# Row maxima beside the mlp in pairs of key blocks, and attention turns of six score tiles

## The chip, the cores and the metric

The kernel runs on one core of one Trainium2 chip. A core has five engines with a queue each: PE (TensorE, matrix products; its weight loads are shown apart as PEld), DVE (VectorE), ACT (ScalarE), POOL (GpSimd) and SP (SyncE, which here only starts transfers). Each queue runs in order, and they wait for one another through semaphores. PE writes to PSUM, 128 partitions by 8 banks of 512 f32 numbers. The metric is the device time of one execution in microseconds (us); lower is better. The inputs are f32. Most products are done in fp32r with each operand split into a high part (h) and a remainder (l), as three products hh + hl + lh.

## The reference

```python
x = A_x                                              # 1 x 2048 x 448
g = sigmoid((x * gate_w).sum(-1, keepdims=True))
# a: attention of 16 heads of 28
qkv = (x @ wqkv) split into q, k, v by heads
a = softmax(q @ k.T * 28 ** -0.5) @ v  (all heads side by side)  @ wo
# b: an mlp per token, 448 -> 1792 -> 448
y = layernorm(x)
b = gelu_tanh(y @ w1 + b1) @ w2 + b2
out = g * a + (1 - g) * b                            # 1 x 2048 x 448
```

Both halves read the same x; B_x is not used.

## The kernel before

Sizes: S = 2048 tokens in NC = 4 chunks of CH = 512 (TPC = 4 tiles of 128 each); 16 heads in NG = 4 sets of four; NF = 14 blocks of 128 hidden units. A "group" n = 0..15 is a set of heads and a chunk of queries, (g, c) = divmod(n, 4). The four heads j of a set lie on partitions 32j to 32j + 27, so that matmuls of four heads use four separate row groups of PE and can run side by side.

Stages, in PE's order, which is written out by hand for the whole kernel:
- q, k, v (L168, L184) to DRAM as high part and remainder; LayerNorm's statistics, turned to rows by two transposes (`ln_turn`, L212 to L214), each copied by DVE before it is stored.
- the mlp: for each chunk c, `mlp1(f)` for 14 blocks (11 products of 512 columns each, L451; then the gelu on ACT twice, L454 and L455, for the rounded and the full value, and the remainder `hl` on POOL, L456), then `mlp2(c, i)` for four token tiles (14 x 3 products of 448 columns, L463 to L466, a copy on ACT and a store). Its sums lie in banks 0 and 1. Weights are fetched, copied on ACT and subtracted during chunk 0 (`load_w1`, `load_w2`); the next chunk's normalised x is made by `ln_apply` on POOL and ACT. The order on ACT, DVE, POOL and SP is the scheduler's in this stage.
- the attention, in which all four other engines keep the order of the text: 256 steps (16 groups by 16 key tiles of 128) of four score tiles (four heads, each 128 keys by 512 queries), 1024 units u in turns of U = 5. `scores` (L620) issues three products for each of the first three units (banks 0 to 2, L629), an exp over the three banks (L634, ACT), then the same for the other two (banks 3 and 4). Behind them stand the p·v products (L658, f32, bank 7) of the steps whose four exps were in earlier turns: one step, or two in every fourth turn. After a group's last step `finish` divides by the softmax's sum; from the last set of heads on, `project` (L525 to L527) and `gated` follow in bank 6.

The exp needs the maximum of each row of scores beforehand; it is subtracted as a 29th row of the score products. The class `RowMax` computes it: per group 64 matmuls of 28 rows (128 queries by 512 keys, high parts only, L321) into a bank, and `reduce_max` on DVE, one or two banks at a time (L301, L303). A `close` turns a group's result (16 columns) and stores it to `ms`; `load_qm(n)` brings it into the 29th row and first issues whatever is missing. The 1040 units (16 x 65) are spread over PE's order by `Filler`: 476 of them beside the mlp, six at a time in banks 2 to 7 ("a visit"), counted out in slots of one product; the rest in the attention, up to three a turn in banks 5 and 6. In the mlp the keys lie in `khr`, loaded block by block with four transfers (`load_khr`, L381).

Of the kernel before, what the change touches and what calls it, by code (L numbers as in the profile page):

```python
# [30 lines left out]
MLP_MAX = 476  # L31
MLP_G = MLP_MAX // 260
MG = 6
FS = 4
LQ = 12
STEPS = (2, 5, 7, 8, 9, 10)
# [3 lines left out]
def kernel(ctx: ExitStack, tc: tile.TileContext, xt, wqk, wv, wo, xk, w1, b1, w2, b2,  # L40
# [7 lines left out]
    sel = const.tile([P, P], F32, name="sel")  # L48
# [16 lines left out]
    one_t = const.tile([S // P, P], F32, name="one_t")  # L65
    nc.vector.memset(one_t, 1.0)
    nc.sync.dma_start(ones, one_t)

# [15 lines left out]
    def staged(width):  # L84
        return my.tile([P, CH], F32, name="r", bufs=3)[:, :width]

    def load_w1(f):
        r = staged(CH)
        nc.sync.dma_start(r, w1[f].rearrange("p t x -> p (t x)"))
# [20 lines left out]
    def ln_fetch(c, t):  # L110
        lnx[c, t] = staged(CH)
        nc.sync.dma_start(lnx[c, t], xt[t, :, c * CH:(c + 1) * CH])
# [12 lines left out]
    with tc.tile_pool(name="qx", bufs=2) as qx, tc.tile_pool(name="qo", bufs=3) as qo, \  # L125
# [67 lines left out]

        def ln_stats(i):
            x = qx.tile([P, 2, D], F32, name="bxr")
            nc.sync.dma_start(x, xk[2 * i:2 * i + 2].rearrange("t p d -> p t d"))
# [22 lines left out]
        for c in range(NC):  # L219
            for m in range(NM):  # L220
                if c == 0:
                    if m + 1 < NM:
                        load_wqk(m + 1)
                    if m == 1:
                        for t, s in ((ident, ident_d), (sel, sel_d), (b1s, b1)):
# [11 lines left out]
                if c == 0 and m in (3, 5):  # L237
                    ln_stats(m // 4)
                if c == 1 and m == 1:
                    ln_rows(0, TPC)  # L240
                if c == 1 and m == 5:
                    ln_turn(0, TPC)
                if c == 1 and m == 6:
                    ln_load(0)
                if c == 1 and m >= 4 or c == 2 and m < 3:
                    ln_stats(m - 2 if c == 1 else m + 5)
                if c == 2 and m in (0, 1, 2, 4):
                    ln_fetch(0, (0, 1, 2, 2, 3)[m])
                if c == 2 and 3 <= m < 6 or c == 3 and m == 0:
                    ln_apply(0, m - 3 if c == 2 else 3)  # L250
# [4 lines left out]
                if c == 3 and m < 3:  # L255
# [513 lines left out]
```

## Time and profile before

| | |
|---|---|
| median of 3 runs | 1148.91 us (1144.49 to 1150.78) |
| the profiled execution | 1146.98 us |
| its span (first to last instruction) | 1145.2 us |
| granted TensorE clock, mean | 0.991 |
| PE busy | 1116.6 us, 98%, 8136 matmuls |
| DVE, ACT, POOL busy | 731.6, 635.9, 331.0 us |
| first and last L451 | 126.5 and 444.0 us |
| first L629, last L658 | 486.5 and 1130.1 us |

Durations below are of that one execution. A row of the groups reads: line, engine, operation, output<-input by the program's names with shapes and count; then busy us in all and mean ns of one; then the engine's idle us just before it and what ended them. A row of the timeline: start, duration, engine, line, operation, names, shapes, number merged into the row, and in brackets the idle time before. Matmul ends are modelled, and a matmul of f32 operands (L658) leaves two records, so that a step of four heads shows eight. What the engines are worth in a stage is read from stretches of that stage.

### The profile page before, as it was taken

The page shows a single profiled execution, that of the slowest core. Times are in us where ns is not written, and L with a number is a line of the kernel's source. Part 1 is how long each engine was busy: PE and PEld are TensorE (multiplying, and loading weights), DVE is VectorE, ACT ScalarE, POOL GpSimd, SP SyncE. Part 2 cuts the span into 40 slices and gives each one's busy share as a digit, 9 for nine tenths or more (in the row PEclk, how much of TensorE's full clock was granted, in tenths as well). Part 3 has the DMA queues.
Part 4 walks back from the last instruction along what each step waited for, and adds up shares of the span by engine and source line. Part 5 has one row for each costly group of instructions (what it writes and reads, how often), then busy time and mean ns, then how long its engine had stood idle before and what let it go on. Part 6 is the DMA issues. An engine that isn't in the chain of part 4 may idle for free.

```text
span 1145.2 us, 19823 instructions
## 1 busy us (share of the span) xinstructions
PE 1116.6 (98%) x8136; PEld 678.4 (59%) x8136; DVE 731.6 (64%) x1033; ACT 635.9 (56%) x668; POOL 331.0 (29%) x355
## 2 busy tenths in 40 slices
PE   6999989999999999989999999999999999999998
PEld 4778867777767777744444444444444444454556
DVE  3433287888878888666676766676676667646103
ACT  5324551132033032067887878878787887848463
POOL 4043367146044032011123012311222123444250
PEclk9999999999999999989999999999999999999999
DMA  8878643002100014062101211111121003002201
GB/s 269 277 217 303 208 141 88 25 9 68 47 23 18 25 30 114 25 168 72 30 12 36 52 40 40 36 27 39 31 64 36 18 19 91 12 25 68 66 26 49
DMA packets 53519, 84.35 MB, mean 74 GB/s; under 512 B 8676, under 2 KB 28660, under 8 KB 52628
## 3 DMA queue, kind: packets, MB, share of 16 engines
q1 hardware_dynamic: 49236, 76.96, 22.5%
q0 software_dynamic: 4192, 6.12, 2.1%
q8 instruction: 64, 1.05, 0.4%
q14 instruction: 27, 0.22, 0.1%
HBM read 56.40 MB, written 26.49 MB: 72 GB/s over the span
## 4 chain that ended last, share of the span: by engine, by line
PE 89%; DMA 4%; POOL 3%; DVE 2%; issue 1%; ACT 1%; SPq 0%; POOLq 0%; ACTq 0%; DVEq 0%
PE bank L658 22%; PE bank L629 20%; PE bank L321 15%; PE bank L451 10%; PE bank L168 4%; PE bank L466 4%; PE bank L463 4%; PE bank L464 4%; PE bank L184 2%; PE bank L525 1%; DMA bxr<-in_xk 1%; PE bank L526 1%; PE bank L527 1%; DMA xraw<-in_xt 1%; POOL hl L456 1%
## 5 line engine op out<-in xcount | busy, mean ns | idle before, releaser
L634 ACT ACTIVATE pt<-bank 128x1536 f32<-128x1536 f32 (+1 forms) x410 | 484.6, 1234 | 155.9 <-PE bank L629 155.9
L301 DVE TENSOR_REDUCE mx<-bank 128x1 f32<-128x512 f32 x624 | 413.4, 687 | 174.9 <-PE bank L321 161.0
L658 PE MATMUL bank<-pt,vg 128*32 128x512 f32 x2048 | 263.7, 606 | 0.0
L303 DVE TENSOR_REDUCE mx<-bank 128x2 f32<-128x1024 f32 x200 | 235.4, 1219 | 41.1 <-PE bank L321 41.0
L321 PE MATMUL bank<-khi,qd 28*128 28x512 f32 x512 | 241.6, 479 | 0.3 <-DVE mx L301 0.2
L321 PEld LDWEIGHTS bank<-khi,qd 28*128 28x128 f32 x512 | 92.3, 181 | 148.3 <-DVE mx L301 107.0
L629 PE MATMUL bank<-qh,klo 28*128 28x512 f32 x1024 | 179.0, 395 | 0.0
L629 PE MATMUL bank<-qh,khi 29*128 29x512 f32 x768 | 161.8, 484 | 0.3 <-ACT h L469 0.3
L451 PE MATMUL bank<-y,w1f 128*128 128x512 f32 x616 | 153.2, 400 | 0.6 <-ACT h L455 0.6
L451 PEld LDWEIGHTS bank<-y,w1f 128*128 128x128 f32 x616 | 113.8, 190 | 36.1 <-issue 12.5
L629 PE MATMUL bank<-ql,khi 28*128 28x512 f32 x768 | 133.6, 393 | 0.0
L456 POOL TENSOR_TENSOR hl<-h,hh 128x512 fp32r<-128x512 f32 x56 | 72.5, 1295 | 172.0 <-ACT h L455 160.8
L658 PEld LDWEIGHTS bank<-pt,vg 128*32 128x32 f32 x2048 | 45.7, 108 | 84.6 <-issue 83.1
L629 PEld LDWEIGHTS bank<-qh,klo 28*128 28x128 f32 x1024 | 90.2, 186 | 4.2
L321 PE MATMUL bank<-khr,qd 28*128 28x512 f32 x512 | 80.7, 467 | 7.3 <-DVE mx L303 4.2
L541 POOL DMA_DIRECT2D lt<-ob x15 | 10.8, 723 | 265.7 <-DVE ob L540 265.7
L466 PE MATMUL bank<-w2h,hl 128*128 128x448 f32 x224 | 85.1, 380 | 1.9 <-POOL hl L456 1.9
L469 ACT ACTIVATE h<-bank 128x448 f32<-128x448 f32 x16 | 8.7, 543 | 140.4 <-PE bank L466 140.4
L629 PEld LDWEIGHTS bank<-qh,khi 29*128 29x128 f32 x768 | 63.3, 183 | 36.8 <-ACT pt L634 32.1
L463 PE MATMUL bank<-w2h,hh 128*128 128x448 f32 x224 | 84.7, 378 | 0.3 <-ACT hh L454 0.3
L454 ACT ACTIVATE hh<-bank,b1s 128x512 fp32r<-128x512 f32 x56 | 38.4, 685 | 81.9 <-PE bank L451 81.8
L464 PE MATMUL bank<-w2l,hh 128*128 128x448 f32 x224 | 82.3, 368 | 0.0
(100 smaller groups left out, 1237.0 us busy)
## 6 DMA issues: line engine op xcount, KB each, us to landing
qk<-hl SPq DMA_DIRECT2D x28, 512.0 KB
xraw<-in_xt SPq DMA_DIRECT2D x16, 256.0 KB
vs<-vt SPq DMA_DIRECT2D x16, 256.0 KB
r<-in_xt SPq DMA_DIRECT2D x16, 256.0 KB
rc<-rls POOLq DMA_DIRECT2D x60, 64.0 KB, 2.2
bxr<-in_xk SPq DMA_DIRECT2D x8, 448.0 KB
r<-in_w SPq DMA_DIRECT2D x14, 256.0 KB
gbs<-h SPq DMA_DIRECT2D x16, 224.0 KB
```

What stands on the lines that cost most here:

```text
L168: nc.tensor.matmul(ps, a, b, start=(i == 0), stop=(i == len(ops) - 1))
L301: nc.vector.reduce_max(self.mx[:, c0:c0 + 1], bank[:, b0], axis=AX)
L303: nc.vector.reduce_max(self.mx[:, c0:c1 + 1:c1 - c0], bank[:, b0:b1 + 1], axis=AX)
L321: nc.tensor.matmul(bank[:, b], self.qds[self.n][r, i * P:(i + 1) * P], khi[self.n // NC][r, k * 512:(k + 1) * 512], start=True, stop=True)
L451: nc.tensor.matmul(ps, a, b, start=(i == 0), stop=(i == len(ops) - 1))
L456: nc.gpsimd.tensor_sub(hl[f], h, hh[f].bitcast(F32))
L463: nc.tensor.matmul(a, hh[f][:, sl], w2h[f], start=(f == 0), stop=False)
L464: nc.tensor.matmul(a, hh[f][:, sl], w2l[f], start=False, stop=False)
L466: nc.tensor.matmul(a, hl[f][:, sl], w2h[f], start=False, stop=(f == NF - 1))
L629: nc.tensor.matmul(bank[:, u % U], a[r, k * P:(k + 1) * P], b[r], start=(i == 0), stop=(i == 2))
L634: nc.scalar.activation(t, bank[:, b:b + len(units)], AF.Exp, scale=SCALE)
L658: nc.tensor.matmul(pv[32 * j:32 * j + 32, :], vg[n // NC][:, k, 32 * j:32 * j + 32], probs.pop(4 * step + j), start=(k == 0), stop=(k == N ...
```

## The change

- `RowMax.visit` replaces the visits in the mlp. The keys are taken two blocks of 512 at a time, a and b: `load_khr` now puts K_a - K_b in the place of block a (two transfers per head into a staging buffer of the pool `rl` and into `khr`, and a subtraction on POOL) and K_b in the place of b. For three units at a time, three matmuls give a - b in banks 2 to 4 and three give b in banks 5 to 7. ACT computes relu(a - b) into a buffer of `rl` (three buffers), and one DVE instruction forms b + relu(a - b), which is max(a, b), and its maximum along the row. A group is 32 such pairs and a close.
- NX = 11 of the 16 groups (704 of 1024 maxima) are done so, in visits of three units (MG) from block FS = 6 of the first chunk on. The other five stay in the attention as before, one bank (6) at a time.
- The attention's turns have six units, two triples, in banks 0 to 5, with at most two row maxima each: one ahead of the first triple and one behind the second's products; one only in the turn after a projection (`projected`). STEPS, which counts turns after a group's end, is adapted, and six buffers hold the exps.
- In `mlp1` the gelu runs once, and DVE copies it to `hh`.
- In the mlp ACT, DVE, POOL and SP now keep the order of the text. Weights and x have fetches apart from their splits, in two staging buffers (four until chunk 0 is over).
- `ln_turn` makes both transposes before one copy; statistics are fetched earlier; loads of `sel`, `ones` and of the keys of sets 1 to 3 (`load_khi`) move.

The core of the diff:

```diff
-MLP_MAX = 476
-MLP_G = MLP_MAX // 260
-MG = 6
-FS = 4
+NX = 11
+MG = 3
+FS = 6
 LQ = 12
-STEPS = (2, 5, 7, 8, 9, 10)
+STEPS = (1, 3, 5, 6, 7, 8)
...
+    stages, turn = [my.tile([P, CH], F32, name=f"s{i}") for i in range(2)], 0
+
+    def staged(width=CH):
+        nonlocal turn
+        turn += 1
+        return stages[turn % len(stages)][:, :width]
+
+    wraw = {}
+
+    def fetch_w1(f):
+        wraw[1, f] = staged()
+        nc.sync.dma_start(wraw[1, f], w1[f].rearrange("p t x -> p (t x)"))
+
+    def split_w1(f):
+        r = wraw.pop((1, f)).rearrange("p (t x) -> p t x", t=4)
         t = mw1.tile([P, 8, P], F32R, name=f"w1f{f}")
         w1h[f], w1l[f] = t[:, 0:4], t[:, 4:8]
-        r = r.rearrange("p (t x) -> p t x", t=4)
         nc.scalar.activation(w1h[f], r, AF.Copy)
         nc.gpsimd.tensor_sub(w1l[f], r, w1h[f].bitcast(F32))
 
-    def load_w2(f):
-        r = staged(D)
-        nc.sync.dma_start(r, w2[f])
+    def fetch_w2(f):
+        wraw[2, f] = staged(D)
+        nc.sync.dma_start(wraw[2, f], w2[f])
+
+    def split_w2(f):
+        r = wraw.pop((2, f))
         nc.scalar.activation(w2h[f], r, AF.Copy)
         nc.vector.tensor_sub(w2l[f], r, w2h[f].bitcast(F32))
...
-                r = qw.tile([b - a, P], F32, name=f"rows{a}{n}")
                 nc.tensor.transpose(ps[:b - a, n * P:(n + 1) * P], mr[:, n, a:b], ident)
-                nc.vector.tensor_copy(r, ps[:b - a, n * P:(n + 1) * P])
-                nc.sync.dma_start(lns[n * NT + a:n * NT + b], r)
-
+            r = qw.tile([b - a, 2, P], F32, name=f"rows{a}")
+            nc.vector.tensor_copy(r, ps[:b - a, :2 * P].rearrange("p (n i) -> p n i", n=2))
+            for n in range(2):
+                nc.sync.dma_start(lns[n * NT + a:n * NT + b], r[:, n])
...
+            self.ks = 2 if n < NX else 4
...
+            self.left = [[(i, k) for k in range(self.ks if n < NG * NC else 0) for i in range(TPC)] for _ in range(4)]
+
+        def pick(self, rows):
+            most = max(range(4), key=lambda j: (len(self.left[j]), -j))
+            j = max(rows, key=lambda j: len(self.left[j])) if rows else most
+            return j if self.left[j] else most
+
+        def ended(self):
+
+            self.last = mpool.tile([P, 4 * TPC], F32, name="mf")
+            nc.vector.reduce_max(self.last, self.mx[:, :4 * TPC * self.ks].rearrange("p (a k) -> p a k", k=self.ks), axis=AX)
+            self.begin(self.n + 1)
+
+        def visit(self, first, n):
+
+            got = []
+            for b in range(n):
+                left = sum(len(x) for x in self.left)
+                if self.last is not None and left <= 26:
+                    self.done += 1
+                    self.close(bank[:, first + b])
+                    continue
+                if not left or self.n == NX:
+                    break
+                self.done += 1
+                j = self.pick(None)
+                i, k = self.left[j].pop(0)
+                got.append((b, j, i, k))
+                if left == 20:
+                    self.load(self.n + 1)
+            for half in range(2):
+                for b, j, i, k in got:
+                    r = slice(32 * j, 32 * j + DH)
+                    nc.tensor.matmul(bank[:, first + half * n + b], self.qds[self.n][r, i * P:(i + 1) * P],
+                                     khr[r, (2 * k + half) * CH:(2 * k + half + 1) * CH], start=True, stop=True)
+            for b, j, i, k in got:
+                rl = rl_pool.tile([P, CH], F32, name="rl", bufs=3)
+                at = (j * TPC + i) * 2 + k
+                nc.scalar.activation(rl, bank[:, first + b], AF.Relu)
+                nc.vector.tensor_tensor_reduce(out=rl, in0=bank[:, first + n + b], in1=rl, scale=1.0, scalar=-3e38,
+                                               op0=OP.add, op1=OP.max, accum_out=self.mx[:, at:at + 1])
+            g, c = divmod(self.n, NC)
+            if c == NC - 1 and (g + 1) * NC < NX:
+                for k in {k for _, _, _, k in got}:
+                    if all(n != k for x in self.left for _, n in x):
+                        load_khr(g + 1, k)
+            if got and not any(self.left):
+                self.ended()
...
-                self.max.issue(2, min(MG, self.upto - self.done))
+                self.max.visit(2, MG)
...
+        a, b = (slice((2 * k + i) * CH, (2 * k + i + 1) * CH) for i in range(2))
+        x = rl_pool.tile([P, CH], F32, name="rl", bufs=3)
+        for j in range(4):
+            r, h = D + (4 * g + j) * DH, slice(32 * j, 32 * j + DH)
+            nc.sync.dma_start(x[h], qk[0, r:r + DH, a])
+            nc.sync.dma_start(khr[h, b].bitcast(F32), qk[0, r:r + DH, b])
+        for j in range(4):
+            h = slice(32 * j, 32 * j + DH)
+            nc.gpsimd.tensor_sub(khr[h, a], x[h], khr[h, b].bitcast(F32))
...
-        while filler.done < min(65 * NG * NC, 65 * (n + 1) + 9):
-            filler.max.issue(5, 1)
+        while filler.max.closed <= n:
+            filler.max.issue(6, 1)
...
-        nc.scalar.activation(hh[f], ps, AF.Gelu_apprx_tanh, bias=b1s[:, f:f + 1])
         nc.scalar.activation(h, ps, AF.Gelu_apprx_tanh, bias=b1s[:, f:f + 1])
+        nc.vector.tensor_copy(hh[f], h)
         nc.gpsimd.tensor_sub(hl[f], h, hh[f].bitcast(F32))
...
+    with tc.manual_schedule(engines={E.SP, E.Pool, E.Activation, E.DVE}):
+        for c in range(NC):
+            for f in range(NF):
+                if c == 0:
+                    if f + 3 < NF:
+                        fetch_w1(f + 3)
+                    fetch_w2(f)
+                    if f == 1:
+                        for k in range(2):
+                            load_khr(0, k)
+                    if f == FS:
+                        filler.spread(nc.sync, NX * 33 - 1, (NC * NF - FS) * 23)
+                mlp1(f)
+                if c == 0:
+                    if f + 2 < NF:
+                        split_w1(f + 2)
+                    if f > 0:
+                        split_w2(f - 1)
             if c == 0:
-                load_w2(f)
-            mlp1(f)
-        if c == NC - 1:
-            m0.close()
-            aq = ctx.enter_context(tc.tile_pool(name="aq", bufs=1, side="right", reuse_waits="tile"))
-            load_khi(0)
-            load_klo(0)
-            load_q(0)
-            load_v(0)
-            load_qm(0)
-        else:
-            ln_load(c + 1)
-        for i in range(TPC):
-            if c + 1 < NC:
-                ln_fetch(c + 1, i)
-                ln_apply(c + 1, i)
-            mlp2(c, i)
+                split_w2(NF - 1)
+                stages[2:] = []
+            if c == NC - 1:
+                m0.close()
+                aq = ctx.enter_context(tc.tile_pool(name="aq", bufs=1, side="right", reuse_waits="tile"))
+                load_khi(0)
+                load_klo(0)
+                load_q(0)
+                load_v(0)
+                load_qm(0)
+                load_khi(2)
+            else:
+                ln_load(c + 1)
+                ln_fetch(c + 1, 0)
+                ln_fetch(c + 1, 1)
+            for i in range(TPC):
+                mlp2(c, i)
+                if c + 1 < NC and i < 3:
+                    ln_apply(c + 1, i)
+                    if i < 2:
+                        ln_fetch(c + 1, i + 2)
+                    else:
+                        ln_apply(c + 1, 3)
...
-    ap = sb("ap", 4)
-    U, UA = 5, 3
+    ap = sb("ap", 6)
+    U, UA = 6, 3
...
-    filler.spread(nc.gpsimd, NG * NC * 65, ((NG * NC - 2) * NT + LQ - 1) * 4 // U)
+    filler.spread(nc.gpsimd, NX * 33 + (NG * NC - NX) * 65, ((NG * NC - 2) * NT + LQ - 1) * 4 // U)
...
-        if most > 0:
-            filler.max.issue(5, 1, [(first[0] + 3) % 4])
+        if early and most > 0:
+            filler.max.issue(6, 1, [(first[0] + 3) % 4])
...
-            if i == 0 and most > 1:
-                filler.max.issue(6, 1, [(first[0] + 1) % 4, (first[0] + 2) % 4])
+        if most > early:
+            filler.max.issue(6, 1, [(first[0] + 2) % 4])
         if last:
             exps(last)
-        if most > 2:
-            filler.max.issue(5, 1, [(first[0] + 1) % 4, (first[0] + 2) % 4])
...
-            scores(units, min(3, filler.due()))
+            scores(units, min(2, filler.due()), not projected)
+            projected = False
...
+                projected = len(acc) > 0 and since >= STEPS[2]
```

More of the change, by code (lines that the diff above doesn't have):

```diff
@@ L306, in issue @@
             for b in range(first, first + n):
-                if self.done >= NG * NC * 65:
+                left = sum(len(x) for x in self.left)
+                if self.last is not None and left <= 56:
+                    reduce()
+                    self.done += 1
+                    self.close(bank[:, b])
+                    continue
+                if not left:
                     break
                 self.done += 1
-                left = sum(len(x) for x in self.left)
-                if self.last is not None and (left <= 56 or self.n == NG * NC):
-                    reduce()
-                    self.close(bank[:, b])
-                    continue
-                most = max(range(4), key=lambda j: (len(self.left[j]), -j))
-                j = max(rows, key=lambda j: len(self.left[j])) if rows else most
-                if not self.left[j]:
-                    j = most
+                j = self.pick(rows)
                 i, k = self.left[j].pop(0)
@@ L470, in mlp2 @@
         nc.sync.dma_start(gbs[c * TPC + i], gb)
[L472 to L498 removed]
+    E = mybir.EngineType
```

105 lines of the change are left out of this document (44 added, 61 removed).

## Prediction

> **What bounds the kernel now.** I read the chain of waits first, then the busy time by stretches, then the groups by form, then the timeline of one stretch in each of the two long stages.
>
> ```profile
> PE 89%; DMA 4%; POOL 3%; DVE 2%; issue 1%; ACT 1%; SPq 0%; POOLq 0%; ACTq 0%; DVEq 0%
> ```
> ```profile
> 250.00:300.00 50.00, 50.00 (x262) 37.77 (x261) 42.41 (x41) 11.15 (x19) 23.94 (x19) 1.00 0.16 51
> 700.00:750.00 50.00, 50.00 (x481) 23.66 (x477) 34.13 (x54) 40.31 (x35) 10.55 (x16) 1.00 0.08 21
> ```
> The columns after the stretch are PE, PEld, DVE, ACT and POOL. PE is never idle in either stage, at full granted clock. Beside it DVE is at 85% in the mlp and ACT at 81% in the attention. By the lines' first and last starts, q, k and v take 0 to 126.5 us, the mlp 126.5 to 486.5, the attention 486.5 to 1130, and the end 15 us.
>
> An attention turn of five score tiles, in the timeline:
> ```profile
> 702.37 0.50 PE L629 MATMUL bank<-qh,khr 29*128 29x512 f32 x3
> 703.15 0.49 PE L629 MATMUL bank<-qh,khr 29*128 29x512 f32 x2
> 703.45 2.37 ACT L634 ACTIVATE pt<-bank 128x1536 f32<-128x1536 f32 x2 [0.35 <-PE bank L629]
> 704.08 1.07 PE L658 MATMUL bank<-pt,vg 128*32 128x512 f32 x8
> 705.07 0.50 PE L321 MATMUL bank<-khi,qd 28*128 28x512 f32 x1
> 706.78 1.92 PE L658 MATMUL bank<-pt,vg 128*32 128x512 f32 x16
> 708.63 0.50 PE L321 MATMUL bank<-khi,qd 28*128 28x512 f32 x1
> ...
> 1090.17 0.51 PE L629 MATMUL bank<-qh,khi 29*128 29x512 f32 x3
> 1092.77 0.50 PE L629 MATMUL bank<-qh,khi 29*128 29x512 f32 x3
> ```
> Triple 0.78 to 0.81 us, pair 0.91, one p·v step (8 records) 0.99, two steps 1.85: turns of 2.70 and, every fourth, 3.56 to 3.63. The last two lines are neighbouring turns without row maxima: 2.60. So a row maximum costs PE at most 0.1 us a turn here: moving it away gains little; turn shape decides.
>
> A visit to the row maxima in the mlp:
> ```profile
> 303.40 0.36 PE L466 MATMUL bank<-w2h,hl 128*128 128x448 f32 x1
> 303.69 0.77 PE L321 MATMUL bank<-khr,qd 28*128 28x512 f32 x6
> 304.22 0.69 DVE L301 TENSOR_REDUCE mx<-bank 128x1 f32<-128x512 f32 x1 [0.32 <-PE bank L321]
> 304.39 0.47 PE L463 MATMUL bank<-w2h,hh 128*128 128x448 f32 x1
> ...
> 307.33 0.36 PE L466 MATMUL bank<-w2h,hl 128*128 128x448 f32 x1
> 307.63 0.73 PE L321 MATMUL bank<-khr,qd 28*128 28x512 f32 x6
> 308.28 0.47 PE L463 MATMUL bank<-w2h,hh 128*128 128x448 f32 x1
> ```
> From the mlp product before a visit to the one behind it pass 0.99 and 0.95 us instead of 0.20: a visit costs PE 0.76 us, in line with everything else.
>
> **The change, part by part.** Prices from these groups:
> ```profile
> L301 DVE TENSOR_REDUCE mx<-bank 128x1 f32<-128x512 f32 x624 | 413.4, 687 | 174.9 <-PE bank L321 161.0 <-PE bank L629 1.2
> L171 DVE TENSOR_TENSOR hl<-bank,hl 128x512 fp32r<-128x512 f32 x28 | 19.3, 688 | 37.3 <-ACT hl L170 36.8 <-DMA vs<-vt 0.3
> L170 ACT ACTIVATE hl<-bank 128x512 fp32r<-128x512 f32 x28 | 16.5, 590 | 29.5 <-PE bank L168 29.3 <-DMA qk<-hl 0.2
> L187 DVE COPY zall<-bank 128x1 f32<-128x1 f32 x16 | 2.5, 156 | 22.3 <-ACT vt L186 22.3
> ```
>
> 1. More visits, +31 us. Matmuls for one block stay one each, but 11 groups of queries are now done in the mlp: 352 pairs and 10 closes, three a visit, 121 visits instead of 80. Each is again six 28-row matmuls, two deep. 41 x 0.76 = 31.
>
> 2. The banks of a visit, +25 us (0 to 45). Banks 2 to 4 hold a - b, 5 to 7 hold b. Counted from a visit's first matmul, a bank is readable at 0.53 (303.69 to 304.22); relu, priced as the copy L170, ends at 1.12; three fused passes at 0.69 (L171, the same operands) follow. In the built program each is two DVE instructions, the pass and one of 128x1 that fetches the accumulator. The trace has none; between nothing and 0.22 (the 128x16 reduction L337), I take 0.12, below the 0.156 of L187, which reads PSUM. Bank 7 is free at 1.18 + 3 x 0.69 + 2 x 0.12 = 3.49, and 0.06 later PE sees it; the sixth matmul wants it 0.28 into the next visit (one product of 0.23 behind the first, and the small steps between). So two visits must stand 3.27 apart. 9.5 slots of 0.23 (mlp1) or 0.20 (mlp2) and 0.76 give 2.93 and 2.70. A delay also postpones the next visit, so half of the gap is lost per visit: 0.17 and 0.29, 0.23 x 121 = 28, less what item 3 absorbs. PE, in order, holds every mlp product behind that sixth matmul. The second gelu (56 x 0.69 on ACT) goes and a 128x512 copy on DVE comes (56 x about 0.42, from the 128x448 cast L593 at 0.389): both lie beside PE, DVE staying at about 85 to 90%; without that cover the copies would cost 24.
>
> 3. Reloading the keys, +16 us (0 to 30). load_khr now takes one of three rl buffers, issues eight DMAs instead of four (0.40 each: four in 1.59 at L385), waits 2.1 for landing (qd's median) and makes four subtractions on POOL, whose time doesn't fall with fewer partitions (L122, 64x512, 1.287): some 10 us. The third relu of the next visit needs that buffer 5 to 6 us earlier; behind it in ACT stand the other relus and gelus, behind them the banks, and PE. Four reloads (two halves, two sets of heads), about 4 us each beyond slack; the scheduler's order before had no such buffer.
>
> 4. Text order, +14 us (0 to 35). After mlp2(c,2) ACT has two y copies in a row, the second behind three POOL operations of 1.29 that follow the first; the next visit's relus stand behind both: three times 2.5 = 8. In c = 0 w1's remainder follows gelu, the DVE copy behind up to three passes, and hl on POOL: 4.1 to 5.4 us after a product ends, wanted at 3.9: 6 for the stretch.
>
> 5. Turns of six, -29 us (-63 to -20). PE alone: 0.81 + 0.90 + 0.99 or 1.85, alternately, for six tiles: 6.26 per twelve. Now ACT: exp of a triple starts 1.07 after its turn (702.37 to 703.45 and its kind), runs 1.45 and follows another at 1.35. In a one-step turn the second exp runs from 2.42 to 3.87, while PE wants its banks at 2.70 + 0.81 = 3.51: it starts at 3.93, and the two turns take about 6.69. 85.3 x 6.69 = 571. Before: 51.2 fours of turns at 3 x 2.70 + 3.60 = 11.7 give 600. One row bank instead of two: reduced by 1.95 when wanted at 1.90, counted as nothing.
>
> 6. A run on one bank, +25 us (5 to 28). Five groups of 65 remain for 156 turns, 2.08 a turn, but a turn takes at most two, or one after a projection. In the built program load_qm(15) therefore issues 20 row maxima behind one another, all on bank 6: 0.53 + 0.69 + 0.06 = 1.28 each, since the next matmul waits for the reduction. Scores and p·v stand behind them on PE.
>
> 7. ln_turn now makes both transposes before one copy: the second waited 4.0 us for the first's copy, -4. Fewer constants, earlier fetches: nothing, as PE waits little there. The key loads that move (five DMAs each on SP, khi(1) to k = 8, khi(2) ahead of the attention, khi(3) to k = 12) are wanted groups of 16 steps later, and SP's queue is nearly empty in the attention: nothing; without that, PE would wait for each about 4 us (1.59 of issue, 2.1 of landing).
>
> Sum: 31 + 25 + 16 + 14 - 29 + 25 - 4 = +78. The profiled execution has a span of 1145.2 and took 1147.0; the median of the runs shown is 1148.9. I predict 1147 + 78 = **1225 us**.
>
> [...]
>
> **Rivals.**
> - *The mlp's waits are hidden* (relus run ahead, buffers come in time): items 2 to 4 cost about 10 rather than 55: 1180. For it: ACT has 78% idle in the mlp. Against: these are waits of order, not of load.
> - *Faster*: as that, and ACT never holds PE in the attention, so item 5 is -63 and the run costs 15: 31 + 10 - 63 + 15 - 4 = -11, 1136. It decides if an exp frees its banks by 3.51. Against: the same 3.87 follows from two trace durations.
> - *The fused pass is half as fast*. A reduction's 512 further elements cost 0.53 (1.219 of L303 less 0.687), so a pass takes 1.22, with its fetch 1.34; a visit then needs 4.0 on DVE and 0.2 of copies against 2.93: 121 x 1.27 = 154 in place of items 2 to 4: 1324. Against: L171, PSUM and SBUF in, has no such penalty; but it has no accumulator.
>  [...]
>
> **How the numbers follow.** Forecast 0.58 (1195 to 1265 by its own bounds), hidden waits 0.22 (1150 to 1195), faster 0.12, half rate 0.08. Items 1 and 6 are nearly certain and alone undo item 5. The range 1150 to 1285 leaves out the faster case and most of half rate. A difference under 0.5% can't be told from none; the low edge of hidden waits gives 0.04 to that. Faster 0.12, same 0.04, slower 0.84.
>
> **What would show it.** Right: 121 visits of about 1 us, a fused row near 0.7 with a small second row, PE waiting for it at the sixth matmul; mlp near 435 to 450 us; two attention turns in 6.7; a gap of 25 us late. Wrong: an mlp near 385, turns of 6.3, or a fused row over 1.1.

## The result, and the profile after

The changed kernel takes 1252.76 us (median of four runs, 1248.91 to 1260.63) where the kernel before takes 1148.20 (four runs beside it): a ratio of 1.0922, 95% interval 1.086 to 1.0984. The forecast was 1225 us, range 1150 to 1285. The profiled execution after has a span of 1247.1 us against 1145.2. By the lines' first and last starts in the two traces:

| us | before | after | difference | forecast |
|---|---|---|---|---|
| q, k, v | 126.7 | 121.1 | -5.6 | -4 |
| mlp | 359.8 | 452.2 | +92.4 | +86 |
| attention, first L629 (after: L711) to last p·v | 643.6 | 654.2 | +10.6 | -4 |
| end | 15.1 | 19.6 | +4.5 | 0 |

The page of the changed kernel, its engines and the chain of waits:

```profile
PE 1145.0 (92%) x8136; PEld 671.0 (54%) x8136; DVE 566.0 (45%) x1287; ACT 769.6 (62%) x896; POOL 355.7 (29%) x360
PEclk9999789899989989998999989999999999997799
PE 56%; issue 14%; ACT 10%; DMA 8%; POOL 7%; DVE 3%; SPq 1%; ACTq 0%; POOLq 0%; DVEq 0%
```

PE has the same 8136 matmul records as before, but is idle for 102.1 us of the span instead of 28.6. DVE lost 166 us of work, ACT gained 134; neither was the limit. The chain, 89% PE before, now runs for 28% through ACT, DMA, POOL and DVE. What PE waits for, before and then after (us in total, times, longest):

```profile
PE bank L321 <- DVE mx L303: 4.2, 2, 2.4
PE bank L212 <- DVE rows L213: 4.0, 2, 3.6
```
```profile
PE bank L391 <- DVE mx L373: 25.7, 26, 2.2
PE bank L516 <- POOL w1f L96: 18.1, 6, 14.2
PE bank L711 <- ACT pt L716: 17.5, 66, 0.4
PE bank L340 <- ACT rl L345: 12.1, 4, 5.9
...
PE bank L340 <- DMA qd<-qk: 5.5, 1, 5.5
```

In order: row maxima that wait for their one bank (14.9 us in the run of maxima at 1132 us, 10.8 us in seven waits before it); w1's remainder, late on POOL in chunk 0; the exp that holds a bank in the attention, 66 times a little; the relu late on ACT in four visits; one wait for queries. The run, w1's remainder, the exp and the relu were in the forecast; the seven waits and the wait for queries were not. The two stretches that were shown of before, and the one with the run:

```profile
250.00:300.00 50.00, 50.00 (x256) 33.61 (x254) 35.97 (x112) 32.99 (x60) 17.79 (x14) 1.00 0.12 34
700.00:750.00 50.00, 46.28 (x428) 19.61 (x420) 18.71 (x29) 37.47 (x28) 12.17 (x17) 0.93 0.17 40
1150.00:1200.00 50.00, 41.90 (x299) 20.21 (x299) 8.78 (x15) 23.03 (x17) 9.38 (x12) 0.80 0.11 34
```

The mlp between its waits is as full as before; the last column but two shows a granted clock below 1 in the other two (0.93, 0.80). The clock records of the two traces hold only 1.0 and 0.5: 109.8 us at half in ten stretches, against 23.7 in five before (the last of each reaches past the span's end).

A visit in the changed mlp, the counterpart of the one at 303.69:

```profile
269.04 0.74 PE L340 MATMUL bank<-khr,qd 28*128 28x512 f32 x6
269.57 1.58 ACT L345 ACTIVATE rl<-bank 128x512 f32<-128x512 f32 x3
270.20 0.69 DVE L346 CUSTOM_DVE_ANT_0 rl<-bank,rl 128x512 f32<-128x512 f32 x1 [0.30 <-ACT rl L345]
270.82 0.08 DVE L346 DVE_READ_ACCUMULATOR2_ANT mx<- 128x1 f32 x1
270.82 0.68 DVE L346 CUSTOM_DVE_ANT_0 rl<-bank,rl 128x512 f32<-128x512 f32 x1
271.43 0.08 DVE L346 DVE_READ_ACCUMULATOR2_ANT mx<- 128x1 f32 x1
271.43 0.69 DVE L346 CUSTOM_DVE_ANT_0 rl<-bank,rl 128x512 f32<-128x512 f32 x1
272.04 0.08 DVE L346 DVE_READ_ACCUMULATOR2_ANT mx<- 128x1 f32 x1
272.17 0.50 PE L340 MATMUL bank<-khr,qd 28*128 28x512 f32 x3
```

A fused pass has 0.69 us and its accumulator's row 0.08, but three passes start 0.615 apart, the fetch included: the next pass begins beside it. The banks are free 3.08 us after the visit's first matmul, and PE, back at 3.13, doesn't wait.

Two places where it does wait. Chunk 0 (131 to 145 us), and a token tile of the second product (235 to 241 us); the bracket is the idle time before:

```profile
131.15 10.85 POOL L452 TENSOR_TENSOR khr<-rl,khr 28x512 fp32r<-28x512 f32 x8 [3.55 <-DMA khr<-qk]
142.08 1.26 POOL L521 TENSOR_TENSOR hl<-h,hh 128x512 fp32r<-128x512 f32 x1
143.30 1.26 POOL L96 TENSOR_TENSOR w1f<-s,w1f 128x512 fp32r<-128x512 f32 x1
144.61 5.72 PE L516 MATMUL bank<-y,w1f 128*128 128x512 f32 x14 [14.18 <-POOL w1f L96]
```
```profile
235.28 0.62 ACT L123 ACTIVATE y<-s 128x512 fp32r<-128x512 f32 x1
235.98 1.29 POOL L125 TENSOR_TENSOR y<-s,y 128x512 fp32r<-128x512 f32 x1 [8.13 <-ACT y L123]
237.23 1.28 POOL L121 TENSOR_TENSOR s<-s,lnr 128x512 f32<-128x512 f32 x1
238.58 1.26 POOL L122 TENSOR_TENSOR s<-s,lnr 128x512 f32<-128x512 f32 x1
239.88 0.63 ACT L123 ACTIVATE y<-s 128x512 fp32r<-128x512 f32 x1 [3.97 <-POOL s L122]
240.41 3.22 ACT L345 ACTIVATE rl<-bank 128x512 f32<-128x512 f32 x6
241.05 2.75 PE L340 MATMUL bank<-khr,qd 28*128 28x512 f32 x6 [2.98 <-ACT rl L345]
```

In the first, eight subtractions of the keys wait for a transfer and take 10.85 us; the remainder of w1, which PE needs next, stands behind them in POOL's text order. Of PE's 14.18 us (from 130.44 on) only 0.7 lie before the first subtraction starts. In the second, ACT's second y copy waits for three POOL operations, and the relus of two visits wait behind that copy. With each comes a stretch of half clock: 17.1 us from 132.4 on, of which 12.2 lie within the pause and 4.9 behind it, and 6.8 us from 241.6 on, all behind the pause.

### The profile page after: what moved, and what is told of

Read it like the earlier page. It is cut to its first block, busy times and chain, and to the rows that moved or that the text cites. A ratio compares the mean times of both kernels' runs of the same rounds, so it can differ in the third digit from the quotient of the medians.

```text
span 1247.1 us, 21039 instructions
## 1 busy us (share of the span) xinstructions
PE 1145.0 (92%) x8136; PEld 671.0 (54%) x8136; DVE 566.0 (45%) x1287; ACT 769.6 (62%) x896; POOL 355.7 (29%) x360
## 4 chain that ended last, share of the span: by engine, by line
PE 56%; issue 14%; ACT 10%; DMA 8%; POOL 7%; DVE 3%; SPq 1%; ACTq 0%; POOLq 0%; DVEq 0%
PE bank L738 12%; PE bank L516 10%; PE bank L711 9%; ACT pt L716 9%; PE bank L340 7%; PE bank L391 4%; PE bank L531 4%; PE bank L528 4%; PE bank L529 3%; DMA lt<-ob 2%; DMA xraw<-in_xt 2%; DVE mx L373 1%; PE bank L607 1%; POOL w1f L96 1%; PE bank L608 1%
## 5 line engine op out<-in xcount | busy, mean ns | idle before, releaser
L716 ACT ACTIVATE pt<-bank 128x1536 f32<-128x1536 f32 x342 | 470.6, 1447 | 180.2 <-PE bank L711 180.1
L373 DVE TENSOR_REDUCE mx<-bank 128x1 f32<-128x512 f32 x320 | 220.4, 689 | 297.6 <-PE bank L391 216.1
L346 DVE CUSTOM_DVE_ANT_0 rl<-bank,rl 128x512 f32<-128x512 f32 x352 | 225.2, 687 | 130.5 <-ACT rl L345 125.1
L345 ACT ACTIVATE rl<-bank 128x512 f32<-128x512 f32 x352 | 186.5, 599 | 127.5 <-PE bank L340 122.6
L516 PE MATMUL bank<-y,w1f 128*128 128x512 f32 x616 | 164.1, 412 | 18.1 <-POOL w1f L96 18.1
L711 PE MATMUL bank<-qh,klo 28*128 28x512 f32 x1024 | 156.9, 396 | 0.0
L391 PE MATMUL bank<-khr,qd 28*128 28x512 f32 x256 | 132.2, 516 | 22.5 <-DVE mx L373 21.6
L711 PE MATMUL bank<-qh,khi 29*128 29x512 f32 x768 | 139.0, 473 | 13.7 <-ACT pt L716 13.3
L340 PE MATMUL bank<-khr,qd 28*128 28x512 f32 x704 | 105.4, 461 | 18.1 <-ACT rl L345 12.1
L391 PEld LDWEIGHTS bank<-khr,qd 28*128 28x128 f32 x256 | 48.3, 189 | 135.0 <-DVE mx L373 82.4
L711 PE MATMUL bank<-ql,khi 28*128 28x512 f32 x768 | 118.7, 393 | 0.0
L623 POOL DMA_DIRECT2D lt<-ob x15 | 10.8, 718 | 332.0 <-DVE ob L622 305.3
L340 PEld LDWEIGHTS bank<-khr,qd 28*128 28x128 f32 x704 | 49.2, 187 | 67.9 <-issue 34.5
L711 PEld LDWEIGHTS bank<-qh,klo 28*128 28x128 f32 x1024 | 81.8, 188 | 5.5
L711 PEld LDWEIGHTS bank<-qh,khi 29*128 29x128 f32 x768 | 56.7, 184 | 41.3 <-ACT pt L716 39.3
```

The costliest lines, as they stand in the source:

```text
L340: nc.tensor.matmul(bank[:, first + half * n + b], self.qds[self.n][r, i * P:(i + 1) * P], khr[r, (2 * k + half) * CH:(2 * k + half + 1) * ...
L345: nc.scalar.activation(rl, bank[:, first + b], AF.Relu)
L346: nc.vector.tensor_tensor_reduce(out=rl, in0=bank[:, first + n + b], in1=rl, scale=1.0, scalar=-3e38, op0=OP.add, op1=OP.max, accum_out=se ...
L373: nc.vector.reduce_max(self.mx[:, c0:c0 + 1], bank[:, b0], axis=AX)
L391: nc.tensor.matmul(bank[:, b], self.qds[self.n][r, i * P:(i + 1) * P], khi[self.n // NC][r, k * 512:(k + 1) * 512], start=True, stop=True)
L516: nc.tensor.matmul(ps, a, b, start=(i == 0), stop=(i == len(ops) - 1))
```

## The experiments

Each ratio is against runs of the kernel before on the same chip. The theory at the start: the mlp's loss is order on POOL and ACT. The rival: it is the buffers.

**Keys staged in `khr` itself, no `rl` buffer.** 

```diff
-        x = rl_pool.tile([P, CH], F32, name="rl", bufs=3)
+        x = khr[:, a].bitcast(F32)
```


> The key reload stages K_a in khr itself and holds no rl buffer; the four subtractions on POOL stay. Theory A (item 3 of the prediction: the third relu waits for the buffer): four waits of 4 us go, about 16 us less than the changed kernel's 1252.8, near 1236. Theory B (POOL is the cost: the subtractions stand in front of w1's remainders and of the y copies' operands): no gain, 1245 to 1256, and the 14.6 us gap of PE near 130 us stays.

1250.62 us, ratio 1.0905 (1.0866 to 1.0944): the buffer that item 3 charged costs nothing that can be told. The 14 us gap in chunk 0 is unchanged (14.2).

**The same, and one subtraction over 128 partitions instead of four over 28.**

```diff
+        if g == k == 0:
+            nc.gpsimd.memset(khr.bitcast(F32), 0.0)
-        for j in range(4):
-            h = slice(32 * j, 32 * j + DH)
-            nc.gpsimd.tensor_sub(khr[h, a], x[h], khr[h, b].bitcast(F32))
+        nc.gpsimd.tensor_sub(khr[:, a], x, khr[:, b].bitcast(F32))
```


> As e1, and one subtraction over 128 partitions replaces four over 28: POOL's share of a reload falls from 5.2 to 1.3 us, in the first load from 10.9 to 2.6. Theory B: the 14.6 us gap near 130 us shrinks to under 6 us, the 17 us of half clock behind it go or shrink, and part of the gap near 444 us goes: 1222 to 1235. Theory A: no further gain over e1.

1243.99 us, ratio 1.0852 (1.0814 to 1.0891). POOL it is, but the number missed: the reload at 440 to 470 us became 8 us shorter, the gap in chunk 0 only 14.2 to 11.5 us. What holds POOL there in this run is mostly the transfers. The one subtraction of a block must wait for all eight of them and starts at 136.66, where the first of the four small ones needed two and started at 131.15; and the clearing of `khr`, 1.81 us on POOL, now stands ahead of them. So the run doesn't price the eight operations of chunk 0 by themselves.

**The y copies apart**: `ln_apply(c + 1, 3)` a token tile later.

```diff
-                if c + 1 < NC and i < 3:
+                if c + 1 < NC:
                     ln_apply(c + 1, i)
                     if i < 2:
                         ln_fetch(c + 1, i + 2)
-                    else:
-                        ln_apply(c + 1, 3)
```


> The fourth tile's ln_apply follows mlp2(c, 3), so ACT no longer has two y copies in a row. Theory (item 4): the PE gaps of 3 to 6 us near 238, 347 and 462 us go, and with each the 6.8 us of half clock that follows: 3 x (5 + 3) = 24 us less, 1226 to 1236; at most 1 us per chunk is lost where mlp1's last products wait for y. Rival (the relus would be late anyway, as DVE and ACT are busy): within 6 us of 1252.8.

1236.89 us, ratio 1.0778 (1.0739 to 1.0818): most of what the theory said, its time just missed. The gaps at 238 and 347 us are gone, with the half clock behind them: the second products of chunks 0 and 1 fell from 59.1 and 58.3 to 52.1 and 51.7 us. In chunk 2, where the keys are reloaded as well, a gap of 3.2 us stays, so the saving is 16 us.

**Twelve groups in the mlp** (`NX = 12`, `load_khi(3)` ahead of the attention, `load_khi(2)` at k = 12).

> NX = 12: 64 more maxima beside the mlp, four groups left for the attention, 1.7 a turn, so that no run on bank 6 should stand ahead of load_qm(15). Theory: the run (27 us, near 1136 to 1163) and the half clock in and behind it (3 to 4 us) go, 11 more visits cost 9: about 21 us less, 1228 to 1236. Rival (the run only shows waits for ACT or p.v that come anyway): 1255 to 1262.

1244.36 us, ratio 1.0847 (1.0813 to 1.0881), between the two expectations. The run is gone and the attention takes 615.9 us instead of 654.2, but the mlp takes 485.1, 33 more for 11 visits: the median visit is 1.09 us instead of 0.99, so at this density PE does lose time in an ordinary visit, and the long waits grew (8.7 us at 441).

**The mlp's order left to the scheduler**: the `manual_schedule` around the mlp taken away.

> The mlp of the changed kernel with the order on ACT, DVE, POOL and SP left to the scheduler, as before the change; all else as changed. Theory (text order makes the long gaps: the second y copy on ACT behind three subtractions on POOL, hl and w1's remainders behind the eight key subtractions in chunk 0): the gaps over 2.5 us at 130, 238, 347, 440 and 462 us and the half clock behind them shrink, the mlp falls from 452 to 405 to 425 us and the time to 1205 to 1225 us. Rival (the gaps come from what the visits themselves need, three relus and three fused passes in turn): the gaps stay or move, the mlp stays over 440 us, 1240 to 1260 us, or more if the scheduler puts a relu behind something longer.

1234.35 us, ratio 1.0776 (1.075 to 1.0802): between the two expectations, so neither is confirmed. The gap in chunk 0 shrinks from 14.2 to 4.5 us, but six others of 1.0 to 2.6 us stand in the mlp in place of the old ones, and half clock stays at 109 us in all. The mlp is 15 us shorter.

**Turns of five in the attention**, all else as changed.

```diff
-    U, UA = 6, 3
+    U, UA = 5, 3
-STEPS = (1, 3, 5, 6, 7, 8)
+STEPS = (2, 5, 7, 8, 9, 10)
-            scores(units, min(2, filler.due()), not projected)
+            scores(units, min(3, filler.due()), True)
```
(and `scores` as before the change, with banks 5 and 6 for the maxima)

> The changed kernel with the attention's turns, row maxima and steps of before (five units, banks 5 and 6, up to three maxima a turn). The mlp stays at 452 us. Theory (turns of six gain 29 us, and the run of 20 maxima with its half clock costs 27 + some 17): four turns take 11.7 us again, so the attention gains 29 us, and loses the run, some 30 to 44: attention 640 to 655 us, in all 1238 to 1254 us, so that the new turns with their run are worth nothing. Rival (the run is the price of spreading 325 maxima, not of the turns): a run stays, and the time rises to 1275 to 1285 us.

1229.78 us, ratio 1.0739 (1.0712 to 1.0766): below both expectations, and by the ratios 21 us faster than the changed kernel. Attention 633.2 us, 10.4 under the kernel before, with 239 row maxima fewer in it. From 64 units' score products to the next 64 pass 37.7 us on the median (13 stretches up to unit 832), with turns of six 36.3, so the new turns do gain, but less than their run costs:

| unit | before | after | turns of five |
|---|---|---|---|
| 0 to 832, us | 497.0 | 481.8 | 488.6 |
| 832 to 896 | 49.1 | 45.7 | 47.6 |
| 896 to 960 (the run) | 48.5 | 79.7 | 48.1 |
| 960 to 1024 | 46.5 | 44.5 | 46.5 |

**p·v between the two triples of a turn.**

```diff
         exps(first)
+        between()
         for i in range(3):
             for u in last:
```
(`between` issues the p·v products of exps of two turns earlier, which stood behind `scores`)

> The changed kernel with the p.v products put between the two triples of a turn, for exps of two turns earlier. Theory (ACT's second exp holds the first triple of the next turn, two turns 6.69 us where PE's own work is 6.27): two turns take 6.25 to 6.35 us, 85 x 0.4 = 34 us less: attention 615 to 625 us, time 1215 to 1225 us. Rival (PE's own work with its weight loads is already 6.6): two turns stay at 6.6 to 6.7 us and the time at 1245 to 1255 us. The run of 20 maxima stays by both.

1357.64 us, ratio 1.1845 (1.1818 to 1.1873): both expectations were wrong. Rows of one turn:

```profile
802.75 0.50 PE L391 MATMUL bank<-khr,qd 28*128 28x512 f32 x1
...
803.77 0.69 DVE L373 TENSOR_REDUCE mx<-bank 128x1 f32<-128x512 f32 x1 [1.73 <-PE bank L711]
...
804.51 0.50 PE L391 MATMUL bank<-khr,qd 28*128 28x512 f32 x1 [0.82 <-DVE mx L373]
```

With the p·v products moved, the turn's second row maximum and the first of the next have nothing between them, and both want bank 6: PE waits 0.82 us a turn, and turns take 3.70 us with one p·v step and 4.57 with two. So it doesn't test what it was made for. It does show that the changed turn lives on its p·v products standing between two uses of its one row bank.

**All in one** (own staging, one subtraction, y copies apart, twelve groups, p·v between).

> All in one: keys staged in khr itself with one subtraction a block, the y copies apart, twelve groups beside the mlp, p.v products between the triples. If the savings add (8.8, 13.7, 8.4 and 34 us from 1252.8) 1188 us; as denser visits leave less room for the other waits, 1185 to 1205 us. Rival (the mlp's waits only change places, so that mending one uncovers the next): 1205 to 1225 us. Faster than the kernel before, 1147 us, by neither.

1289.24 us, ratio 1.1251 (1.1218 to 1.1285): the p·v part spoils the attention here too (684.2 us). The mlp, which that part doesn't touch, takes 457.1 us instead of the 485.1 of twelve groups alone: there the mends add.

**Seven groups in the mlp** (448 maxima, as many as before the change), turns of five, own staging, one subtraction, y copies apart (`NX = 7`, `load_khi(1)` ahead of the attention, `load_khi(2)` at k = 8).

> Seven groups beside the mlp (as many row maxima as the kernel before has there, 448 against 455), in the new form, 77 visits; the other nine groups in the attention with turns of five as before the change; keys staged in khr with one subtraction a block, y copies apart. Theory (what costs is that more maxima are put beside the mlp: 44 more visits of 0.76 us and no room between visits for a late ACT or POOL step): visits are again some 4.4 us apart and the mlp falls to 370 to 385 us (360 before, and the gap in chunk 0 with its half clock), attention 640 to 650 us, q, k, v -5: 1155 to 1172 us. Rival (the form costs: relu on ACT and a fused pass hold PE at each visit whatever their number): mlp over 400 us, 1185 to 1205 us.

1193.80 us, ratio 1.0385 (1.0362 to 1.0409). The total lies in the rival's range, but the rival's reason for it doesn't hold: the mlp, which it put over 400, takes 374.0 us, in the range expected, 14.2 over the kernel before. The first product of chunk 0 alone is 18.5 us over (67.1 against 48.6), so all the rest is 4 us under it, and a visit has 0.981 us on the median (before 0.978). PE is full there:

```profile
250.00:300.00 50.00, 50.00 (x256) 36.64 (x255) 27.32 (x82) 25.84 (x47) 20.13 (x16) 1.00 0.12 37
300.00:350.00 50.00, 50.00 (x258) 36.80 (x258) 27.07 (x81) 26.66 (x50) 18.31 (x15) 1.00 0.15 43
```

What was overlooked is in the attention, 679.9 us where 640 to 650 were expected: 585 units over 188 turns are 3.11 a turn where a turn takes three, and 20 maxima again pile up ahead of `load_qm(15)` (82.4 us in the units 896 to 960).

**Pauses in the kernel before**, to price the half clock by itself.

```diff
             nc.tensor.matmul(a, hh[f][:, sl], w2h[f], start=(f == 0), stop=False)
+            if f == 7:
+                for _ in range(((2, 4, 6, 8), (3, 5, 7, 10))[c % 2][i]):
+                    nc.gpsimd.tensor_copy(hh[f], hh[f].bitcast(F32))
```


> The kernel before with sixteen pauses of PE in the mlp, one in each token tile of the second product: 2 to 10 in-place copies of one hh block on POOL (0.61 us each) between two products that read it, so pauses of about 1.5, 2, 2.7, 3.3, 3.9, 4.5, 5.1 and 6.4 us, each length twice. Theory (a pause of PE past some 2.5 to 3 us is answered with a stretch at half the granted clock): half clock of 3.4 us or more stands behind each pause of 3.3 us and over, none behind those of 2 us and under, some 25 to 60 us of it in all where the kernel before has 24; time 1215 to 1240 us. Rival (the half clock in the changed kernel comes from something else than the pauses, such as the load of DVE, ACT and DMA): no new stretches, mean clock 0.99, time 1200 to 1212 us, which is the pauses alone (90 copies of 0.61 and 16 times some 0.3).

1279.51 us, one run (span 1277.7). Two of the pauses, in PE's timeline, and PE's clock in stretches behind them and between (columns as above):

```profile
556.41 0.47 PE L467 MATMUL bank<-w2l,hh 128*128 128x448 f32 x1 [2.15 <-POOL hh L466]
556.72 0.51 PE L469 MATMUL bank<-w2h,hl 128*128 128x448 f32 x1
557.02 0.58 PE L463 MATMUL bank<-w2h,hh 128*128 128x448 f32 x1
```
```profile
550.00:554.00 4.00, 4.00 (x23) 3.03 (x21) 3.24 (x4) 0.25 (x1) 1.28 (x1) 1.00 0.95 262
557.00:563.00 6.00, 6.00 (x20) 4.35 (x19) 3.49 (x3) 0.00 (x0) 0.00 (x0) 0.50 0.00 0
564.00:569.00 5.00, 5.00 (x31) 3.54 (x29) 3.67 (x4) 0.55 (x1) 0.00 (x0) 1.00 0.12 46
```

PE paused 2.15 us, then worked without a pause at clock 0.50 for 6.8 us: 20 matmuls in 6 us, where 31 fit in 5 at full clock. All sixteen pauses, 2.15 to 13.9 us long, have such a stretch, of 3.4 to 17.1 us. It begins 2.2 to 5.2 us after PE stopped, with thirteen of the sixteen still within the pause; 2.9 to 9.2 us of each lie behind the pause. Whole stretches:

| pause, us | 2.15 | 2.76 | 2.83 | 3.51 | 4.19 | 4.87 | 5.54 | 6.90 | 13.5, 13.9 |
|---|---|---|---|---|---|---|---|---|---|
| half clock in and behind it, us | 6.8 | 3.4 | 3.4 | 6.8, 3.4 | 3.4, 6.8 | 6.8, 10.2 | 6.8, 6.8 | 6.8, 6.8 | 17.1, 17.1 |

(One of 4.91 us has 10.2.) Some pauses came out longer than meant, since POOL had other work ahead of the copies, so the total, which neither expectation met, isn't the test; that the clock follows a pause, without any of the changed kernel's load, is. The span grew by 132.5 us for 90 us of pauses, so 42 us were lost besides. Of the 122 us more of half clock some 37 lie where PE stood anyway and 85 where it worked: about half of the time worked at half clock was lost.

**The transposes first, in the kernel before**: one part of the change alone.

```diff
             for n in range(2):
+                nc.tensor.transpose(ps[:b - a, n * P:(n + 1) * P], mr[:, n, a:b], ident)
+            for n in range(2):
                 r = qw.tile([b - a, P], F32, name=f"rows{a}{n}")
-                nc.tensor.transpose(ps[:b - a, n * P:(n + 1) * P], mr[:, n, a:b], ident)
                 nc.vector.tensor_copy(r, ps[:b - a, n * P:(n + 1) * P])
```


> The kernel before with one part of the change: in ln_turn both transposes before the two copies. Theory (PE waits 3.9 us between the two transposes for the first copy, and runs at half clock for 3.4 us behind it): q, k and v are 4 to 6 us shorter, time 1141 to 1144 us, 0.3 to 0.5% under the kernel before. Rival (the stage is held by the transfers of x and the weights, and the wait goes elsewhere): within 0.1%, 1146 to 1148 us.

1142.74 us (six runs) against 1150.09, ratio 0.9944 (0.9923 to 0.9965): faster than both kernels, and as expected. q, k and v end at 120.8 us instead of 126.7, and the 3.4 us of half clock at 58 us are gone too.

**Eight groups, and chunk 0 in another order**: as seven groups, but the keys fetched in blocks 2 and 3, subtracted in 4 and 5, `khr` cleared in block 0, and the key loads ahead of the attention as in the changed kernel.

> As the run with seven groups, with eight (512 maxima beside the mlp, 520 of 1040 units left for 188 turns of five, 2.77 a turn, under the three that a turn can take), and in chunk 0 the keys' transfers, their subtraction and the clearing of the buffer in five different blocks, so that w1's remainders don't stand behind a subtraction that waits for a transfer. From 1193.8 us: the run of 20 maxima goes (82.4 - 48.5 = 34), eleven visits come (8), the gap of 11.3 us in chunk 0 and the half clock behind it go (some 17): 1145 to 1160 us. So by theory the form itself costs nothing, and what is left of the change, mended, stands level with the kernel before. Rival (each mend uncovers the next wait): the gap in chunk 0 only moves, 1165 to 1185 us.

1165.12 us, ratio 1.0199 (1.0151 to 1.0246), at the edge of the rival. The run is gone (attention 641.5 us) and chunk 0's first product takes 57.7 instead of 67.1, but the reload of the second set's keys now does the same harm at another place:

```profile
318.18 1.26 POOL L455 TENSOR_TENSOR khr<-khr 128x512 fp32r<-128x512 f32 x1 [10.50 <-DMA gbs<-h]
319.40 1.26 POOL L121 TENSOR_TENSOR s<-s,lnr 128x512 f32<-128x512 f32 x1
320.74 1.26 POOL L122 TENSOR_TENSOR s<-s,lnr 128x512 f32<-128x512 f32 x1
322.03 0.63 ACT L123 ACTIVATE y<-s 128x512 fp32r<-128x512 f32 x1 [6.26 <-POOL s L122]
322.57 1.55 ACT L345 ACTIVATE rl<-bank 128x512 f32<-128x512 f32 x3
```

One subtraction behind its transfers (SP issued six of the eight from 313.75 on), two of LayerNorm's steps behind it, the y copy behind those, the relus behind the copy: PE stands 6.1 us (317.92 to 324.06), and the clock is at half for 6.8 us from 321.1 on. The fetch and its subtraction would have to be parted here as well; that wasn't tried.

## Why the prediction was right, point by point

The sign held, and so did the stages and most of the mechanism; the sum was 78 us where the median rose by 105. Of the visible signs named ahead these came: 121 visits of 0.99 us, a fused row of 0.687 and a second of 0.082, an mlp of 452 us (435 to 450 named), two turns in 6.68, a late gap, of 31 us. One didn't: PE waiting at a visit's sixth matmul (item 2; in the median visit it begins 0.01 us behind the fifth). Of the rivals none came as a whole, though what "hidden waits" said of a visit's banks did; the half-rate pass is ruled out by its row (0.687 us, the mean of 352, where that rival had 1.22).

1. *More visits, +31.* Right: 41 more at 0.8 us are 33 (a visit's 0.99 less the 0.20 of a product). By seven groups the new form costs no more than the old one per visit (0.981 us on the median against 0.978); it is the number that costs, since a visit's six matmuls add 0.79 us where an attention turn of before took 2.70 us with row maxima and 2.60 without.
2. *The banks of a visit, +25.* The term that was oversized: close to nothing. The step that failed is the addition of pass and fetch, 3 x 0.69 + 2 x 0.12; three passes with their fetches take 1.92 us instead of 2.31 (270.20 to 272.12), so the sixth matmul finds its bank free. With twelve groups the margin is used up in the second products: a visit there takes 1.16 us on the median instead of 1.03, and its sixth matmul begins 0.43 us behind the first instead of 0.35.
3. *Reloading the keys, +16.* Right in kind, wrong in place. The `rl` buffer, by which it was argued, costs nothing that can be told (1250.62). One subtraction a block instead of four is worth some 7 us (1243.99). In chunk 0's first load, which the item didn't charge, PE's 14.2 us are the eight subtractions, 10.9, and hl and w1's remainder behind them, 2.5. With one subtraction, apart from its transfers, as in the run with eight groups, that gap was gone but for pauses of 1.7, 1.5 and 3.2 us, the last for queries.
4. *Text order, +14.* Mechanism shown, size too small: parting the y copies alone gives 16 us where 8 stood, and in chunk 0, where 6 stood for the stretch, the first product takes 26 us more (74.8 against 48.6), under 2 us of it for two more visits and 5.5 for the wait for queries, which stands in no item. The forecast had counted the three waits of 2.5 us and not what PE loses behind them, and had not put chunk 0's eight subtractions ahead of w1's remainder.
5. *Turns of six, -29.* The pair of turns is 6.68 us, as worked out (6.69); the wait for the exp is there:

```profile
708.75 0.50 PE L711 MATMUL bank<-qh,khi 29*128 29x512 f32 x3 [0.24 <-ACT pt L716]
715.43 0.50 PE L711 MATMUL bank<-qh,khi 29*128 29x512 f32 x3 [0.24 <-ACT pt L716]
```

   Over the first 832 units the gain is 15 us, where 29 x 832 / 1024 = 24 was forecast: PE stands 10.8 us in seven turns, with half clock behind two of them (10.2 us at 579, 6.8 at 736). It waits there for the one row bank, which the forecast counted as nothing. In five of the seven DVE's text order has the softmax's reciprocal ahead of the reduction. By the new STEPS it comes one turn after a group's end instead of two, and there it waits for its transfer; before and after:

```profile
DVE lt L543 <- DMA lt<-ob: 4.7, 4, 2.6
```
```profile
DVE lt L625 <- DMA lt<-ob: 26.0, 15, 4.1
```

   With turns of five, where the old STEPS and a second row bank are back, no such wait stands. And turns of five with as few maxima gain 8 of these 15, which the forecast put down to the turns; beside that 7 us, the run makes the new turns a loss. That ACT alone sets 6.69 wasn't tested by a run; the one made for it met the row bank instead.
6. *The run, +25.* Right, and somewhat more: 20 maxima in 30.8 us (1132.50 to 1163.34), +31 in its stretch. Rows from where the clock falls:

```profile
1135.06 0.50 PE L391 MATMUL bank<-khr,qd 28*128 28x512 f32 x1 [0.78 <-DVE mx L373]
1136.34 0.79 PE L391 MATMUL bank<-khr,qd 28*128 28x512 f32 x1 [0.78 <-DVE mx L373]
1137.91 0.79 PE L391 MATMUL bank<-khr,qd 28*128 28x512 f32 x1 [0.79 <-DVE mx L373]
```

   The first three maxima are 1.28 us apart, as priced; the other seventeen, at half clock, 1.57.
7. *ln_turn, -4.* Right: -5.6 in the stage, and 0.56% by itself.

Not in the sum: the half clock, 86 us more of it in the trace. In these stretches PE is busy for 71.2 us, before for 18.6, so it works in 53 of the 86; by the half that was lost with the pauses (42 of 85 us) that is an estimated 26 us, which lie in the terms above that came out too large. The forecast took the clock as full from two stretches of 50 us; the kernel before has five stretches at half, two of them in its mlp (at 161 and 188 us). That the mlp came out at +92 where +86 stood is thus partly luck: the 25 us of item 2, which aren't there, stand in about for the half clock and chunk 0, which were priced too low. And the end, +4.5 us behind the last p·v: the trace shows the last stores issued by 1240.05 us and the span ending at 1247.1, before by 1142.6 and 1145.2; seven groups have 15.4 us there, eight 20.8. Its cause stays open.

## What to carry to other kernels

Where PE is full, taking work off an engine that isn't the limit gained nothing here (DVE's busy time fell by 166 us, the median rose by 105), and moving PE's own work to a place where it no longer hides beside other matmuls cost its whole length (0.79 us for a visit's six, 0.1 us at most for a turn's maxima in the attention). In the hand-written order here the costly step was the one that waits for a transfer: what stood behind it on its engine, and what waited for that, came late (PE stood 14.2 us in chunk 0, 6.1 us with eight groups); with the fetch two blocks ahead of its use, chunk 0 was left with pauses of 1.7, 1.5 and 3.2 us. And a limit per turn (two or three maxima, one bank) must be held against the number to be done before the rest is priced: 2.08 against 2 and 3.11 against 3 each cost over 30 us (31 and 34).

## What the runs showed of the hardware

- A pause of PE cost more than itself in the mlp: 132.5 us of span for 90 us of pauses put into the kernel before. Half clock comes in multiples of 3.41 us (but for the last stretch of a trace, which its end cuts off: 3.25 us before, 7.43 after), with all sixteen of those pauses, of which the shortest are 2.15, 2.76 and 2.83 us, so the 2.5 to 3 us expected as a lower limit are not shown. In that kernel as it was, one pause of 1.78 us has it behind it and one of 2.39 us has not; what decides there is not shown. Within a trace all stretches begin on one grid of 3.41 us: 21 of 21 in the run with pauses, five of five before, ten of ten after.
- No single long pause was needed: in the run of maxima PE pauses 0.78 us at a time, works 0.50 of every 1.28, and after three of these the clock goes to half for 34.1 us, in the changed kernel; with seven groups a stretch of the same length stands in its run.
- The accumulator's fetch behind a fused pass has a row of 82 ns but adds no time in the changed kernel: passes with it are 0.615 us apart (270.20, 270.82, 271.43), shorter than the 0.687 of a pass's own row.
- On POOL 24 subtractions of 28 x 512 took 1.289 us on the mean in the changed kernel, 15 of 128 x 512 (L637) 1.283 there: the four heads of a block apart take 5.16 us, where the one subtraction over 128 partitions has a row of 1.26 (with eight groups, at 318.18).
